# Issuing the first two weight transfers ahead of GpSimd's scaling of R of the third group, in place of behind it

## The chip, the cores and the metric

The kernel runs on one core of one Trainium2 chip. The metric is the time of one execution on the device, in microseconds (us); the number shown for a kernel is the median of several runs. Beside it stands one profiled execution, whose span runs from its first to its last recorded instruction.

The engines are named as in the profile: PE (TensorE matmul) and PEld (its weight loads), DVE (VectorE), ACT (ScalarE), POOL (GpSimd), SP (SyncE, which here only issues transfers). Each engine takes its own instructions strictly in program order.

## The reference

Two layers, one behind the other. The first is an RWKV-5 recurrence over 4 batches, 8 heads, 768 steps and 48 channels a head; the second is a two-layer network with a smooth ReLU, over 3072 tokens.

```python
# r, k, v: (4, 8, 768, 48); w, u: (8, 48)
for t in range(S):
    cur = einsum('bhd,bhe->bhde', u * k[t], v[t])
    y[t] = einsum('bhd,bhde->bhe', r[t], state + cur)
    state = w * state + einsum('bhd,bhe->bhde', k[t], v[t])
x = y.transpose(0, 2, 1, 3).reshape(3072, 384)
h = x @ w_in                                # 384 x 2048
g = where(h >= 1, h, where(h <= -1, 0, (h + 1) ** 2 / 4))
out = g @ w_out                             # 2048 x 384
```

## The kernel before

**Tiling.** The 768 steps are cut into 6 chunks of 128. A *group* is one chunk of two batches (256 tokens), so there are 12 groups, g = 0 to 11, and two *units* (one batch each) in a group: unit n belongs to group n // 2. The third group is g = 2; its units are 4 and 5. Inside a chunk the recurrence is done as matrices: K and R of a group are scaled by powers of w (steps `Ks` and `Rs`, lines 329 to 337), turned on PE (`T`, line 395), copied out of PSUM (`TT`), multiplied with one another (`A`, line 413) and masked (`AT`, lines 416 to 431). `Sp` (line 439) makes the chunk's addition to the state, `Tm` (lines 483 and 491) adds it, `Y` (lines 448 and 453) makes the output. The term with u goes its own way: `KU` (line 344), `RKU` (351), `usum` (a sum per head, 362 or 364), `V2` (376), and `y` (475) adds it to `Y`. The trace leaves numbers out of names, so the tile of `V2` shows as V in it: `V<-V,diag` at line 376 is `V2`.

The second layer takes the group's y turned (`X`, line 508; `xT`): `mm1` (line 533) multiplies with `w_in` in four quarters of 512 columns, `relu` and `square` (lines 541 and 546, ACT) and `gate` (551, DVE) make the activation, and `mm2` (561) multiplies with `w_out`.

**Order.** Nothing is scheduled by a planner. One table of tokens, `ORDER`, lists every step, and the program is written out in that order; each engine's own sequence is what the table leaves for it. A token such as `Rs.2.0@P:0` is step `Rs` of group 2, from unit 0 of the group on, on GpSimd (`@P`; `@D` is DVE, `@A` ACT), into buffer 0; `~4` puts four idle matmuls on zeros ahead of it on PE, and `warm` is idle matmuls alone. From group 2 on a step such as `Ks` or `V2` covers both units at once. A table line as it stands before the change:

```
Ks.2.0@D:0 A.3:0 Y.2:1~4 AT.1.1:1 Rs.2.0@P:0 Tm.3@D loadV.2.0:0 w_in.0 w_in.1 V2.1.0@P:0 T.5:1~8 ...
```

**Transfers.** K, R and V are loaded by SP, 384 KB for a group (line 311), in rows of 192 bytes. The weights are float32 in DRAM and bf16 on the chip, and GpSimd issues their transfers (line 297 for `w_in`, line 301 for `w_out`): `w_in.0` and `w_in.1` are columns 0 to 511 and 512 to 1023, `w_in.2` the other 1024, and `w_out.0` to `w_out.3` a quarter each. Such an issue takes GpSimd's own time, in line with its arithmetic.

**The steps around the change.** On GpSimd stand here, in this order: the masking of `AT` of unit 0 (line 423), `Rs.2.0`, the issues `w_in.0` and `w_in.1`, `V2.1.0` (group 1's first unit), the masking of `AT` of unit 1, `w_out.0`, `w_in.2`, `V2.1.1`, `KU.2.0`. DVE meanwhile does `V2.0.1`, `Tm` of unit 0, `Ks.2.0`, `Tm` of unit 3, `y.2`, `AT.3.0`. `Rs.2.0` and `Ks.2.0` are read by PE in `T.5` and `T.4`; the first reader of the weights is `mm1.0.0.0` (group 0, first quarter, unit 0), which stands on PE behind `T.5`, `T.4`, `Y.1`, two idle matmuls, `A.5`, `X.1` and `Y.3`.

Of the kernel before, what the change touches and what calls it, by code (L numbers as in the profile page):

```python
# [14 lines left out]
P = 128  # L15
# [23 lines left out]
Rs.0.1@D T.2:1~2 load.K.1.1 A.0:0 load.R.1.1 TT.2@D:1 AT.0.1:3 Sp.1:0 Tm.2@D A.2:1~2 V2.0.0@D:1 KU.1.1@D Rs.1.1@D  # L39
loadV.1.1 RKU.1.1@P AT.0.0 load.R.2.0:1 Ks.1.1@D V.1.1@A T.1:0~2 Tm.1@D usum.0.1@A Y.0:1~16 AT.2.0:0 TT.1@D:0 y.0:1  # L40
T.3:1~7 warm.6.h.2 V2.0.1@D Sp.0:0~4 usum.1.0@A:0 TT.3@A:1 A.1:2 X.0:1~4 Tm.0@D load.K.2.0:1 Sp.3:0 xT.0@A:1
Ks.2.0@D:0 A.3:0 Y.2:1~4 AT.1.1:1 Rs.2.0@P:0 Tm.3@D loadV.2.0:0 w_in.0 w_in.1 V2.1.0@P:0 T.5:1~8 sbf.1@A T.4:2~2
TT.5@A:1 AT.1.0 w_out.0 y.2:1 AT.3.0:2 w_in.2 Y.1:0~4 warm.2.h.0 A.5:1 y.1:2 usum.1.1@D X.1:1~2 Y.3:0~4 AT.5.0:0
TT.4@A:2 V2.1.1@P mm1.0.0.0:2 xT.1@A A.4:0~7 y.3:0 AT.4.0:2 X.2:1~4 load.K.3.0:2 V.2.0@A:1 xT.2@A:0 X.3:0 KU.2.0@P:1
mm1.0.0.1 mm1.0.1.0:0 w_out.2 xT.3@A mm1.0.1.1 RKU.2.0@D:0 usum.2.0@D:1 w_out.1 Sp.5:1 V2.2.0@P:1 mm1.1.1.-1:1
# [611 lines left out]
```

## Time and profile before

| | |
|---|---|
| median of 3 runs | 174.81 us (174.58 to 174.9) |
| the profiled execution | 174.86 us, span 173.1 us, granted clock 1.000 |
| busy, PE / PEld | 164.1 us (95%) / 125.7 us (73%) |
| busy, DVE / ACT / POOL | 137.5 us (79%) / 133.5 us (77%) / 111.3 us (64%) |
| moved by DMA | 28.78 MB, 166 GB/s over the span |

Rows of the timeline and of the chain of waits begin with the start and the duration in us; a bracket behind a row names how long the engine sat idle before it and what ended that. In the groups by line the three durations are the shortest, the median and the longest in ns. On PE a row's end is modelled, and rows overlap by some 0.15 us.

### The profile page before, as it was taken

The page shows a single profiled execution, that of the slowest core. Times are in us where ns is not written, and L with a number is a line of the kernel's source. Part 1 is how long each engine was busy: PE and PEld are TensorE (multiplying, and loading weights), DVE is VectorE, ACT ScalarE, POOL GpSimd, SP SyncE. Part 2 cuts the span into 40 slices and gives each one's busy share as a digit, 9 for nine tenths or more (in the row PEclk, how much of TensorE's full clock was granted, in tenths as well). Part 3 has the DMA queues.
Part 4 walks back from the last instruction along what each step waited for, and adds up shares of the span by engine and source line. Part 5 has one row for each costly group of instructions (what it writes and reads, how often), then busy time and mean ns, then how long its engine had stood idle before and what let it go on. Part 6 is the DMA issues. An engine that isn't in the chain of part 4 may idle for free.

```text
span 173.1 us, 4227 instructions
## 1 busy us (share of the span) xinstructions
PE 164.1 (95%) x1712; PEld 125.7 (73%) x1712; DVE 137.5 (79%) x175; ACT 133.5 (77%) x193; POOL 111.3 (64%) x92
## 2 busy tenths in 40 slices
PE   1989999999999999999999999999999999999992
PEld 1668879876686767686777876877769677778672
DVE  5299989899888699888998888799978795565451
ACT  4588969998659996379997997986848946898920
POOL 6487997707978479978999999999659200000000
DMA  5999999999999989799999998969999905013022
GB/s 115 210 208 232 204 191 200 182 204 213 205 167 188 202 253 201 125 196 246 153 204 205 202 223 175 229 121 207 162 253 127 139 0 140 0 45 140 0 91 91
DMA packets 107367, 28.78 MB, mean 166 GB/s; under 512 B 100946, under 2 KB 106964, under 8 KB 107348
## 3 DMA queue, kind: packets, MB, share of 16 engines
q1 hardware_dynamic: 103888, 25.24, 72.9%
q0 software_dynamic: 3312, 3.15, 11.5%
q8 instruction: 13, 0.21, 0.5%
q10 hardware_dynamic: 148, 0.13, 0.2%
q14 instruction: 6, 0.05, 0.1%
HBM read 20.45 MB, written 4.72 MB: 145 GB/s over the span
## 4 chain that ended last, share of the span: by engine, by line
PE 73%; DVE 9%; DMA 6%; SPq 4%; issue 3%; POOL 2%; ACT 1%; ACTq 0%
PE op L561 34%; PE hp L533 31%; DMA w_in_sb<-in_moe_w_in_dram 4%; SPq L311 4%; DVE gt L551 3%; PE A L413 3%; DMA R<-in_r_dram 2%; PE Y L448 2%; PE Y L453 2%; DVE Rs L334 1%; PE Sp L439 1%; POOL Rs L334 1%; DVE Tm L483 1%; DVE AT L428 1%; ACT sq L546 1%
## 5 line engine op out<-in xcount | busy, mean ns | idle before, releaser
L533 PE MATMUL hp<-xT,w_in_sb 128*128 128x256 bf16 (+1 forms) x600 | 70.1, 268 | 0.6 <-DVE AT L428 0.4
L561 PE MATMUL op<-w_out_sb,gt 128*128 128x384 bf16 (+2 forms) x400 | 69.6, 320 | 0.0
L551 DVE SCALAR_TENSOR_TENSOR gt<-sq,hp 128x1024 bf16<-128x1024 f32 x48 | 57.8, 1215 | 8.9 <-ACT sq L546 8.4
L533 PEld LDWEIGHTS <-w_in_sb 128*128 128x128 bf16 x600 | 55.4, 98 | 9.6 <-DVE gt L551 0.7
L541 ACT ACTIVATE pt<-hp 128x1024 f32<-128x1024 f32 x48 | 48.7, 1017 | 10.3 <-PE hp L533 9.7
L546 ACT ACTIVATE sq<-pt 128x1024 f32<-128x1024 f32 x48 | 50.5, 1058 | 2.9 <-DVE gt L551 2.0
L561 PEld LDWEIGHTS <-gt 128*128 128x128 bf16 x400 | 36.8, 98 | 20.4 <-DVE gt L551 0.5
L428 DVE TENSOR_TENSOR AT<-A,umask 128x1024 bf16<-128x1024 f32 x22 | 26.5, 1219 | 4.1 <-PE A L413 4.1
L351 POOL TENSOR_TENSOR RKU<-R,KU 128x768 f32<-128x768 f32 (+1 forms) x13 | 20.4, 1572 | 10.2 <-DMA R<-in_r_dram 6.3
L344 POOL TENSOR_TENSOR KU<-K,u_bc 128x768 f32<-128x768 f32 (+1 forms) x11 | 17.6, 1600 | 5.2 <-DMA K<-in_k_dram 5.2
L496 POOL TENSOR_TENSOR state<-Tm,wCm 128x384 f32<-128x384 f32 x16 | 16.8, 1053 | 1.6 <-DVE Tm L483 0.8
L334 POOL TENSOR_TENSOR Rs<-Wup,R 128x768 bf16<-128x768 f32 x9 | 16.4, 1826 | 2.1 <-DMA R<-in_r_dram 2.1
L334 POOL TENSOR_TENSOR Ks<-Wdn,K 128x768 bf16<-128x768 f32 x9 | 16.4, 1824 | 1.5 <-PE Sp L439 1.5
L376 POOL TENSOR_TENSOR V<-V,diag 128x768 f32<-128x768 bf16 (+1 forms) x11 | 15.3, 1390 | 2.8 <-DVE diag L364 2.4
L212 ACT COPY oo<-op 128x384 f32<-128x384 f32 x18 | 8.5, 473 | 10.7 <-PE op L561 9.2
L475 DVE TENSOR_TENSOR yy<-Y,V 128x384 bf16<-128x384 f32 x18 | 9.7, 553 | 3.8 <-PE Y L453 3.0
L453 PE MATMUL Y<-V,AT 128*128 128x48 bf16 x192 | 11.0, 183 | 0.3 <-POOL AT L423 0.3
L483 DVE TENSOR_TENSOR Tm<-Sp,state 128x384 f32<-128x384 f32 x16 | 8.8, 552 | 2.9 <-PE Sp L439 2.5
L364 DVE TENSOR_REDUCE diag<-RKU 128x16 f32<-128x768 f32 (+1 forms) x12 | 10.5, 879 | 0.0
L453 PEld LDWEIGHTS <-AT 128*128 128x128 bf16 x192 | 9.4, 96 | 1.5 <-issue 0.5
L216 ACT CAST V<-VF 128x768 bf16<-128x768 f32 (+1 forms) x11 | 8.1, 739 | 0.7 <-DMA VF<-in_v_dram 0.7
L448 PE MATMUL Y<-state_bf,RT 128*128 128x96 bf16 x72 | 8.5, 204 | 0.0
(85 smaller groups left out, 143.8 us busy)
## 6 DMA issues: line engine op xcount, KB each, us to landing
out_dram<-oo SPq DMA_DIRECT2D x11, 384.0 KB, 3.5
R<-in_r_dram SPq DMA_DIRECT2D x10, 384.0 KB, 4.4
K<-in_k_dram SPq DMA_DIRECT2D x10, 384.0 KB, 6.0
VF<-in_v_dram SPq DMA_DIRECT2D x10, 384.0 KB, 5.2
w_out_sb<-in_moe_w_out_dram POOLq DMA_DIRECT2D x4, 384.0 KB, 8.3
K<-in_k_dram SPq DMA_DIRECT2D x4, 192.0 KB, 3.7
R<-in_r_dram SPq DMA_DIRECT2D x4, 192.0 KB, 3.5
VF<-in_v_dram SPq DMA_DIRECT2D x4, 192.0 KB, 3.8
```

What stands on the lines that cost most here:

```text
L334: engines[e].tensor_mul(of_unit(dst, j0, j1)[:, :, :, :D], rep(tab, j1 - j0), of_unit(tiles[what, g], j0, j1))
L344: engines[e].tensor_mul(of_unit(tiles["KU", g], j0, j1), of_unit(tiles["K", g], j0, j1), rep(u_bc, j1 - j0))
L351: engines[e].tensor_mul(of_unit(tiles["RKU", g], j0, j1), of_unit(tiles["R", g], j0, j1), of_unit(tiles["KU", g], j0, j1))
L376: engines[e].tensor_mul(tiles["V2", g][:, hs, :], tiles["V", g][:, hs, :], tiles["diag", g][:, hs].unsqueeze(2).to_broadcast([P, hs.stop - ...
L428: nc.vector.tensor_mul(t.rearrange("p i n t -> p (i n) t"), tiles.pop(("A", n)).rearrange("p i n t -> p (i n) t"), umask.unsqueeze(1).to_b ...
L453: nc.tensor.matmul(t[:, 2 * p + i, :], tiles["AT", n][:, i, p, :], tiles["V", g][:, j * H + 2 * p + i, :], start=(c == 0), stop=True, skip ...
L496: nc.gpsimd.tensor_mul(states[(g % BP) * UNITS + j], tiles.pop(("Tm", n)), wCm)
L533: nc.tensor.matmul(hp[:, f, cols], w_in_sb[:, i, n0 : n0 + P], tiles["xT", g][:, units, i, :], start=(i == 0), stop=(i == nK - 1), skip_gr ...
L541: nc.scalar.activation(tiles["pt", g, q], tiles["hp", g, q], AF.Relu, bias=0.5, scale=0.5)
L546: nc.scalar.activation(tiles["sq", g, q], tiles.pop(("pt", g, q)), AF.Square, bias=0.0)
L551: nc.vector.scalar_tensor_tensor(out=gt, in0=tiles.pop(("sq", g, q)), scalar=1.0, in1=tiles.pop(("hp", g, q)), op0=ALU.min, op1=ALU.max)
L561: nc.tensor.matmul(t, tiles["gt", g, q][:, f, j * P : (j + 1) * P], w_out_sb[:, n, cols], start=(n == 0), stop=(n == nF - 1),)
```

## The change

The two tokens `w_in.0 w_in.1` move ahead of `Rs.2.0@P:0` in the table; of the 715 tokens in it no other is altered. `Tm.3@D` (DVE) and `loadV.2.0:0` (SP), which stood between, belong to other engines and keep their places there.

```diff
-Ks.2.0@D:0 A.3:0 Y.2:1~4 AT.1.1:1 Rs.2.0@P:0 Tm.3@D loadV.2.0:0 w_in.0 w_in.1 V2.1.0@P:0 T.5:1~8 sbf.1@A T.4:2~2
+Ks.2.0@D:0 A.3:0 Y.2:1~4 AT.1.1:1 w_in.0 w_in.1 Rs.2.0@P:0 Tm.3@D loadV.2.0:0 V2.1.0@P:0 T.5:1~8 sbf.1@A T.4:2~2
```

GpSimd, from the masking of unit 0 to that of unit 1 (`V_411<-V,diag` is `V2.1.0`); the difference of the two programs:

```order
 L423 AFFINE_SELECT AT<-AT 128x1024
+L297 DMA w_in_sb<-in_moe_w_in_dram 128x3x512 x2
 L334 TENSOR_TENSOR Rs<-Wup,R 128x16x48
-L297 DMA w_in_sb<-in_moe_w_in_dram 128x3x512 x2
 L376 TENSOR_TENSOR V_411<-V,diag 128x384
 L423 AFFINE_SELECT AT<-AT 128x1024
```

The two issues and `Rs.2.0` have changed places; what follows them is as it was. DVE over the same stretch, with what each row waits for; it reads alike in both programs (`V_247` is `V2` of group 0, the rows of line 491 are `Tm`, the row of line 334 is `Ks.2.0`):

```order
L475 TENSOR_TENSOR y<-Y,V_247 128x384 [waits DVE_49,PE_49]
L376 TENSOR_TENSOR V_247<-V,diag 128x384 [waits Activation_49]
L491 TENSOR_TENSOR state<-Sp,wCm 128x384 [waits PE_49]
L334 TENSOR_TENSOR Ks<-Wdn,K 128x16x48 [waits DMAHW7_49]
L491 TENSOR_TENSOR state<-Sp,wCm 128x384 [waits PE_49]
L475 TENSOR_TENSOR y<-Y,V_411 128x384 [waits DVE_49,PE_49,Pool_49]
L428 TENSOR_TENSOR AT<-A,umask 128x1024
```

Nothing moved on DVE, and `Ks.2.0` waits for its load of K and for no other engine; `y.2`, two rows on, waits for GpSimd's `V2.1.0`. On PE, ACT and SP too both programs have the same rows.

## The prediction

> **What bounds the kernel now.** I read the page first, then the chain of waits, then the waits of the stretch from 20 to 24.5 us, and last the timelines around the change. From the page, the shares of busy time and the chain by engine; from the chain in order of time, one piece; from the waits, one line:
>
> ```profile
> core 0: 173.1 us, clock 1.000
> PE 164.1 (95%) x1712; PEld 125.7 (73%) x1712; DVE 137.5 (79%) x175; ACT 133.5 (77%) x193; POOL 111.3 (64%) x92
> PE 73%; DVE 9%; DMA 6%; SPq 4%; issue 3%; POOL 2%; ACT 1%; ACTq 0%
> 17.66 6.09 DMA w_in_sb<-in_moe_w_in_dram
> PEld L533 <- DMA w_in_sb<-in_moe_w_in_dram: 0.2, 1, 0.2
> ```
>
> PE is 95% busy and holds 73% of the chain. The chain also runs through 6.09 us of the first weight transfer, issued behind `Rs.2.0`, which makes it look as if every microsecond of an earlier issue were won. The waits say otherwise: PE's weight load stood 0.2 us for this transfer. The chain names who came last; the wait says by how much. So 0.20 us is all that an earlier landing can give directly, however early it is.
>
> **What GpSimd does, and whom it holds up.** The timeline of POOL, then of DVE, then of PE; line 423 is the masking, line 376 `V2`:
>
> ```profile
> 15.89 1.83 POOL L334 TENSOR_TENSOR Rs<-Wup,R 128x768 bf16<-128x768 f32 x1
> 17.66 1.70 POOL L297 DMA_DIRECT2D w_in_sb<-in_moe_w_in_dram  x2
> 19.38 1.14 POOL L376 TENSOR_TENSOR V<-V,diag 128x384 f32<-128x384 bf16 x1
> 20.49 1.08 POOL L423 TENSOR_SCALAR_AFFINE_SELECT AT<-AT 128x1024 bf16<-128x1024 bf16 x1
> 23.25 0.83 POOL L376 TENSOR_TENSOR V<-V,diag 128x384 f32<-128x384 bf16 x1 [0.18 <-DVE diag L364]
> ...
> 12.78 0.55 DVE L376 TENSOR_TENSOR V<-V,diag 128x384 f32<-128x384 bf16 x1
> 17.31 0.82 DVE L376 TENSOR_TENSOR V<-V,diag 128x384 f32<-128x384 bf16 x1
> 18.14 0.56 DVE L491 TENSOR_TENSOR state<-Sp,wCm 128x384 f32<-128x384 f32 x1
> 18.62 1.22 DVE L334 TENSOR_TENSOR Ks<-Wdn,K 128x768 bf16<-128x768 f32 x1
> 20.55 0.56 DVE L475 TENSOR_TENSOR y<-Y,V 128x384 bf16<-128x384 f32 x1 [0.25 <-POOL V L376]
> 21.03 1.22 DVE L428 TENSOR_TENSOR AT<-A,umask 128x1024 bf16<-128x1024 f32 x1
> 26.55 0.95 DVE L351 TENSOR_TENSOR RKU<-R,KU 128x768 f32<-128x768 f32 x1
> ...
> 17.77 0.33 PE L439 MATMUL Sp<-V,Ks 128*128 128x96 bf16 x4
> 20.37 0.39 PE L395 MATMUL T<-ident,Ks 128*128 128x128 bf16 x4
> 20.59 0.39 PE L395 MATMUL T<-ident,Rs 128*128 128x128 bf16 x4
> 21.63 0.37 PE L453 MATMUL Y<-V,AT 128*128 128x48 bf16 x8
> 22.30 0.29 PE L615 MATMUL idle<-zeros 128*128 128x128 bf16 x2 [0.30 <-DVE AT L428]
> 23.79 0.84 PE L533 MATMUL hp<-xT,w_in_sb 128*128 128x128 bf16 x12
> ```
>
> Two things are to be seen. GpSimd has no gap from 15.89 on. And the same `V2` of 128x384 takes DVE 0.55 us at 12.78 and 0.82 us at 17.31, where GpSimd's `Rs.2.0` runs until 17.72; on GpSimd it takes 0.83 us at 23.25 and 1.14 us at 19.38, where DVE's `Ks.2.0` runs until 19.84. So the two get in each other's way where both read two tensors from SBUF. The clearest rows stand later, with what PE does there; from SP's timeline the load of R for group 3, and from the page's transfers its kind:
>
> ```profile
> 27.52 0.37 SPq L311 DMA_DIRECT2D R<-in_r_dram x1
> ...
> R<-in_r_dram SPq DMA_DIRECT2D x10, 384.0 KB, 4.4
> ...
> 39.89 1.82 POOL L351 TENSOR_TENSOR RKU<-R,KU 128x768 f32<-128x768 f32 x1 [6.29 <-DMA R<-in_r_dram]
> 41.68 1.70 POOL L496 TENSOR_TENSOR state<-Tm,wCm 128x384 f32<-128x384 f32 x1
> ...
> 40.16 2.37 DVE L334 TENSOR_TENSOR Rs<-Wup,R 128x768 bf16<-128x768 f32 x1
> 42.45 1.21 DVE L551 SCALAR_TENSOR_TENSOR gt<-sq,hp 128x1024 bf16<-128x1024 f32 x1
> ...
> 42.78 0.81 PE L561 MATMUL op<-w_out_sb,gt 128*128 128x384 bf16 x4
> 43.72 1.48 PE L533 MATMUL hp<-xT,w_in_sb 128*128 128x256 bf16 x12
> 43.71 1.21 PEld L533 LDWEIGHTS <-w_in_sb 128*128 128x128 bf16 x12 [0.51 <-DVE gt L551]
> 45.20 0.65 PE op L561 x4
> ```
>
> DVE's `Rs.3.0` begins 0.27 us behind GpSimd's `RKU.3.0` and ends at 42.53, 0.82 behind that one's end at 41.71: it took 2.37 us where a product of this size takes 0.95 (the row at 26.55). It stood until GpSimd was through. And GpSimd, with its next step ready at 41.7, stood in turn until DVE was through. Whoever begins first keeps the other out to its end, and one that stands waiting gets its turn ahead of the other's next step.
>
> **The change, part by part.** All times are in the profiled execution.
>
> *The issues.* They begin at 15.89 in place of 17.66, 1.77 us earlier, and take 1.70 us: until 17.59. `w_in.0` then lands between 23.75 − 1.77 = 21.98, if its queue is no longer, and 23.75, if it only waits longer behind the loads of SP. Either will do, as the last step shows.
>
> *`Rs.2.0`* moves behind them. DVE's `V2.0.1` now begins first, at 17.31, beside issues alone, for 0.55 us: until 17.86. GpSimd comes free of such a wait about 0.15 us ahead of the row's end on DVE (its `V2` at 19.38 takes 1.14 in place of 0.83, so it really began at 19.69, and `Ks.2.0` ends at 19.84). `Rs.2.0` so runs from 17.71 for 1.83 us, to 19.54. PE reads it at 20.59: this delay in itself costs nothing, since 1.05 us of cover are left of 2.9.
>
> *`Ks.2.0` on DVE* is where it costs. The 0.27 us that `V2.0.1` saves do not help: `Tm` behind it waits for `Sp` on PE, which ends at 17.77 + 0.33 = 18.10, so `Tm` stays at 18.14 and `Ks.2.0` at 18.62. There it now meets `Rs.2.0` in place of the issues, and ends 0.82 us behind it: 20.36 in place of 19.84, +0.52 us.
>
> *What is queued behind.* GpSimd's `V2.1.0` would begin at 19.5 but waits for `Ks.2.0`: 20.36 − 0.15 + 0.83 = 21.04, against 20.52. Both engines behind it: the masking ends at 22.12, so PE's `Y.1` begins at 22.14, not 21.63; and `y.2` on DVE, which already stands 0.25 us for `V2.1.0`, begins at 21.07, so `AT.3.0` ends at 22.77, not 22.25. PE's idle matmuls at 22.30 stand for that `AT`: 22.82. (`T.5` needs `Ks.2.0` at 20.37, just in time; a little lateness there lies inside the wait of `Y.1`.) PE is +0.52 here, and gives back the 0.20 us for the weights at `mm1.0.0.0`: 23.79 + 0.52 − 0.20 = 24.11, later than both landings. Net +0.32 us.
>
> *The bound from above.* `Ks.2.0` took 1.22 us beside issues alone, where 0.95 would be its price alone. I don't know what the 0.27 us are. If an issue adds as much to `V2.0.1`, this ends at 18.13 as before, and all of the above is 0.27 later: +0.59 us. I take +0.43, halfway, as neither row is nearer.
>
> Here a rule of the Trainium skill, "SBUF — State Buffer", section "Who interferes with whom", differs from the row. It says that a DVE instruction with two SBUF inputs contends with a GpSimd instruction that reads SBUF, as a lock held for the whole instruction, and infers that writing transfer descriptors does not collide with it. By that rule the sum would be +0.32, by the row at 18.62 +0.59; the lock itself agrees with the 2.37 us at 40.16.
>
> *Whether it reaches the end.* From 24 to 43 us each step hangs on PE's `A.4` behind `mm1.0.0.0`, and PE, ACT and DVE shift together. But at 43.72 PE waits for DVE's `gate`, which stands behind `Rs.3.0`, which stands behind `RKU.3.0`, which began when R of group 3 landed, at 39.89. That does not hang on PE: DVE may arrive at 40.16 + 0.43 and still end at 42.53. PE's spare time here is between 43.72 − (42.78 + 0.65) = 0.29 and the weight load's 0.51; I take 0.40. So the end moves by the larger of 0.43 − 0.40 = 0.03 and the shift of that landing. The landing came 12.37 us after the issue at 27.52, against a median of 4.4: 8 us of it are queue behind the weights. The issue follows `RKU.2.0` on DVE (26.55 + 0.95) and so is up to 0.43 late (0.32 to 0.59 by the bounds); the queue in front is as long as before. The shift is thus between 0, if the queue sets it, and all of the delay; I take 0.1, near the queue's end, since 8 of 12 us are queue.
>
> **Sum:** −0.20 (weights) + 0.52 to 0.79 (`Ks.2.0`, `V2.1.0`, `AT.3.0`) − 0.40 (absorbed at 43.72), but not less than the landing's shift: +0.1 us. On the profiled execution's 174.86 that is 174.96; on the median, 0.05 below it, 174.9.
>
> **The rivals.** 0.2% is 0.35 us, about what a measurement of this kernel tells from no change.
>
> *Slower: the delay is carried through.* If R of group 3 lands as late as it is issued, or if GpSimd gets `V2.1.0` in ahead of the waiting `Ks.2.0` (0.83 us more for DVE, PE +1.15), the end moves: +0.32 to 0.59 by the first, +0.75 by the second even with 0.40 absorbed. Time 175.2 to 175.6. It decides from a landing over 0.35 us late, or PE over 0.75 late at `mm1.0.0.0`. For it: the issue of that load does hang on DVE. Against it: the 8 us of queue, and the order of turns at 41.7.
>
> *Faster: no collision.* If `Ks.2.0` is not held, it ends at 18.62 + 0.95 = 19.57, `V2.1.0` at 19.38 + 0.83 = 20.21, `AT.3.0` 0.3 us earlier, and the 0.20 us for the weights is won too: PE −0.2 to −0.5. The end follows only as far as R of group 3 lands earlier: 174.3 to 174.6. Against it: three pairs of rows that show the two engines blocking one another.
>
> *Nothing moves:* the weights are sent no earlier, because they stand behind SP's loads. `mm1.0.0.0` is due at 24.11 and they land at 23.75 at the latest, so the time is that of the forecast.
>
> **How the numbers follow.** The forecast, within 0.35 us of before, has 0.51 (its own range 174.5 to 175.15); the slower rival 0.32, since three steps in a row carry the delay and only one wait absorbs it; the faster one 0.17, which includes that the transfers sort themselves better than the rows tell. The range, 174.3 to 175.6, reaches over most of both, and leaves about 2 in 10 out.
>
> **What would show it.** Right: `V2.0.1` 0.55 us; `Rs.2.0` ending at about 19.5; `Ks.2.0` at about 1.75 us in place of 1.22; no wait of PE for the weights; a longer wait of PE at `Y.1` and ahead of the idle matmuls; `mm1.0.0.0` at 24.1 to 24.4; `RKU.3.0` still at about 39.9. The prediction is wrong if `Ks.2.0` is no longer than before, if `RKU.3.0` moves by more than 0.35 us, or if DVE's `Rs.3.0` gets ahead of `RKU.3.0` (then it takes 0.95, and PE's wait at 43.72 goes).

## The result, and the profile after

The changed kernel takes 175.56 us (median of 20 runs, 175.18 to 177.43), the kernel before 174.90 in the same comparison (20 runs, 174.41 to 175.94): a ratio of 1.0053 (95% interval 1.0031 to 1.0075), slower by some 0.5%. The prediction's 174.9 was "no change". The profiled execution of the changed kernel took 176.90 us. It is one of 6 among its 20 with a granted clock of 0.988 to 0.990 and times of 176.6 to 177.4 us; the other 14 lie between 175.2 and 175.7, so the loss is not that of those 6 alone.

From the page of the changed kernel, the busy shares and the clock in 40 slices; ahead of them the span and mean clock:

```profile
core 0: 175.2 us, clock 0.989
PE 165.2 (94%) x1712; PEld 126.8 (72%) x1712; DVE 137.6 (79%) x175; ACT 133.8 (76%) x193; POOL 112.0 (64%) x92
PEclk9999969999999999999999999999999999999999
```

Busy times are within 0.3 us of before on DVE and ACT; PE and PEld are 1.1 us longer, at a lower clock in the sixth slice (21.9 to 26.3 us), and POOL 0.7. The timeline around the change, POOL, then DVE, then PE:

```profile
15.75 1.70 POOL L297 DMA_DIRECT2D w_in_sb<-in_moe_w_in_dram  x2
17.48 1.82 POOL L334 TENSOR_TENSOR Rs<-Wup,R 128x768 bf16<-128x768 f32 x1
19.25 1.15 POOL L376 TENSOR_TENSOR V<-V,diag 128x384 f32<-128x384 bf16 x1
...
17.19 2.52 DVE L376 TENSOR_TENSOR V<-V,diag 128x384 f32<-128x384 bf16 x1
19.64 0.54 DVE L491 TENSOR_TENSOR state<-Sp,wCm 128x384 f32<-128x384 f32 x1
20.11 1.11 DVE L334 TENSOR_TENSOR Ks<-Wdn,K 128x768 bf16<-128x768 f32 x1
...
20.24 0.34 PE L439 MATMUL Sp<-V,Ks 128*128 128x96 bf16 x4 [1.42 <-ACT AT L419]
```

`V2.0.1` on DVE takes 2.52 us, not 0.55. It began 0.29 us ahead of `Rs.2.0`, and yet ended 0.41 behind it: less its own 0.55, it got going at 19.16, 0.14 ahead of the end of the other's row. `Rs.2.0` was ready all that time: its load of R, the last thing that it waited for, had been issued at 10.82 and took 4.7 us to land, so from about 15.5 on nothing but the steps ahead of it on GpSimd kept it. The hand-over then goes on in turn, each time with 0.13 to 0.14: `V2.1.0` on GpSimd (19.25 + 1.15 = 20.40, so going from 19.57, when `V2.0.1` was through at 19.71), then `Ks.2.0` on DVE (ends 21.22, going from 20.27). Before, `Ks.2.0` ended at 19.84.

On PE stands a wait of 1.42 us at the second `Sp`, that of unit 3. The timeline names ACT's `AT` for it; the waits of 15 to 26 us name what the weight load behind the same point waited for:

```profile
PEld L439 <- DVE state L491: 1.6, 1, 1.6
PE Sp L439 <- ACT AT L419: 1.4, 1, 1.4
```

DVE's `state` at line 491 is `Tm` of unit 0, which reads the PSUM tile that this `Sp` writes next. `Tm` stood behind `V2.0.1` in DVE's order: 19.64 in place of 18.14. The windows of this kernel (length, then busy time of PE, PEld, DVE, ACT, POOL, then the clock) show what followed:

```profile
19.00:21.20 2.20, 0.96 (x21) 0.78 (x22) 2.20 (x4) 1.66 (x3) 2.20 (x3) 1.00 1.18 191
21.20:25.00 3.80, 3.80 (x51) 3.70 (x50) 2.12 (x5) 1.74 (x2) 2.47 (x3) 0.55 1.21 188
...
22.00:23.00 1.00, 1.00 (x12) 1.00 (x11) 1.00 (x2) 0.00 (x0) 1.00 (x3) 0.50 1.20 189
```

In this execution PE ran at half its clock for about 3.4 us behind the gap (an estimate: at 0.50 or 1.00 throughout, a mean of 0.55 over 3.80 us takes 3.4 us at 0.50), and `mm1.0.0.0` began at 26.18. There was no wait for `w_in` any more.

### The profile page after: what moved, and what is told of

It reads as the page before. It is cut to its first block, busy times and chain, and to the rows that moved or that the text cites. A ratio compares the mean times of both kernels' runs of the same rounds, so it can differ in the third digit from the quotient of the medians.

```text
span 175.2 us, 4227 instructions
## 1 busy us (share of the span) xinstructions
PE 165.2 (94%) x1712; PEld 126.8 (72%) x1712; DVE 137.6 (79%) x175; ACT 133.8 (76%) x193; POOL 112.0 (64%) x92
## 4 chain that ended last, share of the span: by engine, by line
PE 86%; DVE 4%; ACT 3%; issue 2%; POOL 1%; DMA 1%; ACTq 0%
PE op L561 36%; PE hp L533 33%; PE A L413 4%; PE Y L453 2%; PE Y L448 2%; PE T L395 2%; PE Sp L439 2%; PE T L204 1%; DMA u_row<-in_u_dram 1%; PE ub L249 1%; PE wc L284 1%; PE wb L244 1%; DVE AT L428 1%; DVE gt L551 1%; ACT sq L546 1%
## 5 line engine op out<-in xcount | busy, mean ns | idle before, releaser
L334 POOL TENSOR_TENSOR Ks<-Wdn,K 128x768 bf16<-128x768 f32 x9 | 17.1, 1901 | 1.9 <-PE Sp L439 1.9
L496 POOL TENSOR_TENSOR state<-Tm,wCm 128x384 f32<-128x384 f32 x16 | 16.0, 1006 | 1.9 <-DVE Tm L483 1.2
```

The costliest lines, as they stand in the source:

```text
L334: engines[e].tensor_mul(of_unit(dst, j0, j1)[:, :, :, :D], rep(tab, j1 - j0), of_unit(tiles[what, g], j0, j1))
L496: nc.gpsimd.tensor_mul(states[(g % BP) * UNITS + j], tiles.pop(("Tm", n)), wCm)
```

## The experiments

The first theory of what had happened: `V2.0.1` is held by `Rs.2.0` from the time on at which that stands ready behind the issues, and the loss is what hangs on that. The rivals: DVE came too late, by a fraction of a microsecond, to go first; the issues themselves hold DVE; the order on DVE (`Tm` behind `V2.0.1`) is the loss; the earlier weight traffic is; the lower clock is. To compare traces, the start of `mm1.0.0.0` is counted from the start of GpSimd's masking of unit 0 (line 423), the step ahead of the change. It is 23.79 − 14.83 = 8.96 us in the trace of before.

| kernel | ratio to before [95%] | median | `V2.0.1` | `Ks.2.0` | `mm1.0.0.0` |
|---|---|---|---|---|---|
| changed, again | 1.0024 [1.0002, 1.0045] | 176.03 | 2.53 | 1.11 | 9.89 |
| changed, again_2 | 1.0016 [0.9993, 1.0038] | 175.74 | 2.53 | 1.11 | 9.89 |
| before_again | 0.9992 [0.9962, 1.0021] | 175.17 | 1.37 | 1.11 | 9.93 |
| tm_first | 1.0006 [0.9985, 1.0027] | 175.77 | 0.57 | 1.58 | 9.89 |
| three_issues | 1.0064 [1.0038, 1.0090] | 176.55 | 1.08 | 2.24 | 9.91 |
| rs_late | 1.0004 [0.9972, 1.0035] | 175.84 | 0.56 | 0.95 | 10.01 |
| v2_early | 1.0076 [1.0049, 1.0104] | 176.26 | 3.00 | 0.94 | 10.37 |
| one_ahead | 1.0014 [0.9994, 1.0034] | 175.30 | 1.76 | 1.61 | 9.62 |
| rs_buffer | 0.9975 [0.9952, 0.9998] | 175.12 | 0.55 | 1.73 | 9.25 |

They ran on three chips, on which the kernel before took 175.44 (again, tm_first, three_issues, rs_late), 174.97 (v2_early, v2_w3, slot, one_ahead) and 175.31 us (rs_buffer, before_again, warm, again_2); medians compare only within a chip. The diffs are against the changed kernel.

**The changed kernel once more (again),** unaltered, beside the next three.

> The changed kernel once more, unaltered. In its first profile V2.0.1 on DVE (line 376) takes 2.52 us from 17.19, to the end of Rs.2.0 on GpSimd, Tm of unit 0 waits behind it, and PE stands 1.59 us for Tm's PSUM bank ahead of Sp.3; from 21.2 to 24.3 us the granted clock is 0.5. Theory of the port: the 2.52 us and PE's gap of about 1.6 us stand in every execution, and cost 0.5 to 0.9 us in time by themselves (175.4 to 175.8). Theory of the clock: the loss is the lowered clock, and an execution at clock 1.000 loses nothing against before (174.6 to 175.1). Expected: a profile or runs at clock 1.000 with 175.5 us, and some runs near 176.8 with clock 0.99.

Slower again, by 0.24%. Its profiled execution kept the clock (0.998), which separates the two parts of the loss. GpSimd, DVE, PE with its weight load, and in a fence of its own a piece of the chain from 30 to 45 us:

```profile
18.00 1.82 POOL L334 TENSOR_TENSOR Rs<-Wup,R 128x768 bf16<-128x768 f32 x1
...
17.71 2.53 DVE L376 TENSOR_TENSOR V<-V,diag 128x384 f32<-128x384 bf16 x1
...
20.64 1.11 DVE L334 TENSOR_TENSOR Ks<-Wdn,K 128x768 bf16<-128x768 f32 x1
...
43.88 1.22 DVE L551 SCALAR_TENSOR_TENSOR gt<-sq,hp 128x1024 bf16<-128x1024 f32 x1 [0.77 <-PE op L561]
...
20.77 0.34 PE L439 MATMUL Sp<-V,Ks 128*128 128x96 bf16 x4 [1.34 <-DVE state L491]
...
42.31 2.11 PE L561 MATMUL op<-w_out_sb,gt 128*128 128x384 bf16 x12 [0.20 <-DMA w_out_sb<-in_moe_w_out_dram]
...
45.15 1.21 PEld L533 LDWEIGHTS <-w_in_sb 128*128 128x128 bf16 x12 [0.30 <-DVE gt L551]
```

```profile
34.12 8.15 DMA w_out_sb<-in_moe_w_out_dram
```

The hold on `V2.0.1` and PE's gap are the same to 0.1 us; here the gap's releaser is named as `Tm`. Further on PE waits 0.20 us for the last quarter of `w_out`, which GpSimd issued at 34.12 and which took 8.15 us to land. In the trace of before that issue went out at 32.80, and nothing waited for it. The weight load's wait for `gate`, 0.51 us at 43.71 before, is 0.30 here; and `gate` itself, which waited for nobody before, waits 0.77 us for PE.

**`Tm` ahead of `V2.0.1` on DVE (tm_first).**

```diff
-T.3:1~7 warm.6.h.2 V2.0.1@D Sp.0:0~4 usum.1.0@A:0 TT.3@A:1 A.1:2 X.0:1~4 Tm.0@D load.K.2.0:1 Sp.3:0 xT.0@A:1
+T.3:1~7 warm.6.h.2 Sp.0:0~4 usum.1.0@A:0 TT.3@A:1 A.1:2 X.0:1~4 Tm.0@D V2.0.1@D load.K.2.0:1 Sp.3:0 xT.0@A:1
```

> The changed kernel with Tm.0 ahead of V2.0.1 on DVE, so that what waits for GpSimd's port no longer stands ahead of what PE waits for. If the loss is the way V2.0.1 -> Tm.0 -> PSUM bank -> Sp.3: Tm.0 begins at about 18.0, Sp.3 on PE at about 18.7 (before: 18.77) with no gap over 0.3 us, V2.0.1 is held from about 18.5 to 19.7, Ks.2.0 ends at 20.5 to 20.7, and the time is 174.6 to 175.1, with no run at a lower clock. If the loss comes from the early transfers themselves (their traffic, or Rs.2.0 late for PE), the time stays at 175.4 to 175.7.

PE's gap at `Sp` is gone, but `mm1.0.0.0` comes no earlier. POOL, then DVE, then PE:

```profile
17.51 1.82 POOL L334 TENSOR_TENSOR Rs<-Wup,R 128x768 bf16<-128x768 f32 x1
19.29 1.15 POOL L376 TENSOR_TENSOR V<-V,diag 128x384 f32<-128x384 bf16 x1
21.00 1.21 POOL L423 TENSOR_SCALAR_AFFINE_SELECT AT<-AT 128x1024 bf16<-128x1024 bf16 x1 [0.56 <-ACT AT L419]
...
19.18 0.57 DVE L376 TENSOR_TENSOR V<-V,diag 128x384 f32<-128x384 bf16 x1
19.68 1.58 DVE L334 TENSOR_TENSOR Ks<-Wdn,K 128x768 bf16<-128x768 f32 x1
...
21.32 0.40 PE L395 MATMUL T<-ident,Ks 128*128 128x128 bf16 x4 [0.22 <-DVE Ks L334]
```

`V2.0.1` is through at 19.75, `V2.1.0` at 20.44, `Ks.2.0` at 21.26: counted from the masking, `Ks.2.0` ends at 6.51, as in again (20.64 + 1.11 − 15.24 = 6.51). So PE's gap is one place where the delay shows, not its source. `Rs.2.0`, `V2.0.1`, `V2.1.0` and `Ks.2.0` go one behind the other whatever the order on DVE. Before, `Ks.2.0` had the issues to run beside; now DVE has nothing of this kind for them. The ratio is back to 1.0006, though its interval overlaps that of again. Behind `mm1.0.0.0` the one thing that its trace has ahead of again's is that the last quarter of `w_out`, issued at 33.63, keeps nobody waiting; the run warm below has the same and is slower, so this trace does not explain the ratio.

**A third issue ahead of `Rs.2.0` (three_issues).**

```diff
-Ks.2.0@D:0 A.3:0 Y.2:1~4 AT.1.1:1 w_in.0 w_in.1 Rs.2.0@P:0 Tm.3@D ...
-TT.5@A:1 AT.1.0 w_out.0 y.2:1 AT.3.0:2 w_in.2 ...
+Ks.2.0@D:0 A.3:0 Y.2:1~4 AT.1.1:1 w_in.0 w_in.1 w_out.0 Rs.2.0@P:0 Tm.3@D ...
+TT.5@A:1 AT.1.0 y.2:1 AT.3.0:2 w_in.2 ...
```

> The changed kernel with w_out.0 also issued ahead of Rs.2.0: issues from 15.75 to 18.25, and Rs.2.0 from there to 20.1. V2.0.1 on DVE begins at about 17.2, in the second issue, as in the changed kernel. Theory A (GpSimd's next arithmetic instruction claims the port as soon as its own waits are met, while the one issue ahead of it is still being written; an issue itself holds nobody): the second issue is followed by a third one, so V2.0.1 takes 0.55 us, PE has no gap ahead of Sp.3, and Ks.2.0 at 18.6 is held to 20.1 and ends at about 20.9. Theory B (the writing of a transfer's descriptors holds a DVE instruction with two SBUF inputs): V2.0.1 is held at least to the end of the third issue at 18.25, over 1.0 us, or to the end of Rs.2.0 at 20.1 (3.3 us), and then the time is 176 or more.

POOL and DVE:

```profile
17.57 0.78 POOL L301 DMA_DIRECT2D w_out_sb<-in_moe_w_out_dram  x1
18.37 1.82 POOL L334 TENSOR_TENSOR Rs<-Wup,R 128x768 bf16<-128x768 f32 x1
...
17.31 1.08 DVE L376 TENSOR_TENSOR V<-V,diag 128x384 f32<-128x384 bf16 x1
18.78 2.24 DVE L334 TENSOR_TENSOR Ks<-Wdn,K 128x768 bf16<-128x768 f32 x1
```

`V2.0.1` lost 0.53 us and then went ahead of `Rs.2.0`: it got going at 17.84, 0.27 into the third issue. This fits neither a claim that holds from the first issue on nor free passage beside issues. `Ks.2.0` then met `Rs.2.0` and took 2.24 us, and the last quarter of `w_out`, issued as late as 37.70, held PE as well. Slower by 0.6%.

**Another GpSimd step behind the issues (rs_late):** `V2.1.0`, whose sums ACT has not finished by then, with `Rs.2.0` behind it.

```diff
-... w_in.0 w_in.1 Rs.2.0@P:0 Tm.3@D loadV.2.0:0 V2.1.0@P:0 T.5:1~8 ...
+... w_in.0 w_in.1 Tm.3@D loadV.2.0:0 V2.1.0@P:0 Rs.2.0@P:0 T.5:1~8 ...
```

> The changed kernel with Rs.2.0 behind V2.1.0 on GpSimd: issues from 15.75 to 17.45, then V2.1.0, which has to wait for ACT's sums until about 18.0, then Rs.2.0. Theory A (the next arithmetic instruction claims the port once its own waits are met): at 17.2 the waits of V2.1.0 are not met, so V2.0.1 takes 0.55 us and PE has no gap ahead of Sp.3. Theory B (the issue itself holds DVE): V2.0.1 is held to 17.45 at least, 0.7 to 0.8 us, as Ks.2.0 took 1.22 in place of 0.95 before. Rs.2.0 ends at about 21, so PE's T.5 waits some 0.4 us and the time is 174.8 to 175.4 by either.

POOL, DVE, PE:

```profile
16.23 1.70 POOL L297 DMA_DIRECT2D w_in_sb<-in_moe_w_in_dram  x2
19.17 1.52 POOL L376 TENSOR_TENSOR V<-V,diag 128x384 f32<-128x384 bf16 x1 [1.24 <-ACT RKU L362]
...
17.66 0.56 DVE L376 TENSOR_TENSOR V<-V,diag 128x384 f32<-128x384 bf16 x1
19.05 0.95 DVE L334 TENSOR_TENSOR Ks<-Wdn,K 128x768 bf16<-128x768 f32 x1
...
22.52 0.40 PE L395 MATMUL T<-ident,Rs 128*128 128x128 bf16 x4 [0.86 <-POOL Rs L334]
```

Beside the same two issues `V2.0.1` now runs free, 0.56 us, and `Ks.2.0`, behind them, takes its bare 0.95. So these two issues did not hold `V2.0.1` by themselves; what stood behind them did. The kernel gains nothing by it, as PE waits 0.86 us for `Rs.2.0`, which is late here.

**`V2.0.1` earlier on DVE, ahead of `y.0` (v2_early),** to see whether DVE only came too late.

```diff
-... Y.0:1~16 AT.2.0:0 TT.1@D:0 y.0:1
-T.3:1~7 warm.6.h.2 V2.0.1@D Sp.0:0~4 ...
+... Y.0:1~16 AT.2.0:0 TT.1@D:0 V2.0.1@D y.0:1
+T.3:1~7 warm.6.h.2 Sp.0:0~4 ...
```

> The changed kernel with V2.0.1 one place earlier on DVE, ahead of y.0, so that it begins at about 16.7, some 0.7 us ahead of Rs.2.0, in the first 0.1 us of the second issue. Theory A (GpSimd's next arithmetic instruction claims the port some time into the issue ahead of it, and an instruction of DVE that begins before that goes first): V2.0.1 takes 0.55 to 0.85 us, PE has no gap ahead of Sp.3, and the rest goes as the prediction had it: Rs.2.0 ends at 19.4, Ks.2.0 is held from 18.6 and ends at 20.2 to 20.4, mm1.0.0.0 begins at 24.0 to 24.5, time within 0.2% of before. Rival (DVE with two SBUF inputs is held through the whole run of issues and Rs.2.0, however early it begins): V2.0.1 takes 2.9 us or more, y.0 and Tm.0 wait behind it, and the time is 0.3% to 0.7% above before.

POOL, DVE, PE:

```profile
16.11 1.70 POOL L297 DMA_DIRECT2D w_in_sb<-in_moe_w_in_dram  x2
17.84 1.82 POOL L334 TENSOR_TENSOR Rs<-Wup,R 128x768 bf16<-128x768 f32 x1
...
17.08 3.00 DVE L376 TENSOR_TENSOR V<-V,diag 128x384 f32<-128x384 bf16 x1
...
20.60 0.38 PE L204 MATMUL X<-zeros 128*128 128x128 bf16 x4 [1.66 <-DVE y L475]
```

It began 0.76 us ahead of `Rs.2.0` and was held to that one's end all the same: 17.08 + 3.00 − 0.55 = 19.53, 0.13 ahead of 19.66. Being first on the clock does not help DVE here. The ratio is the second worst, 1.0076.

**As v2_early, and with the last quarter of `w_out` issued ahead of `Ks.3.0` (v2_w3),** to take away the wait for it.

```diff
-... relu.0.2:0 square.0.2:1 Ks.3.0@P:2 KU.3.0@D:1
-... gate.0.3:0 w_out.3 mm1.1.3.-1:0 Rs.3.0@D:2
+... relu.0.2:0 square.0.2:1 w_out.3 Ks.3.0@P:2 KU.3.0@D:1
+... gate.0.3:0 mm1.1.3.-1:0 Rs.3.0@D:2
```

> As v2_early, and w_out.3 is issued ahead of Ks.3.0 on GpSimd, 1.8 us earlier. In the profile of the changed kernel on this chip PE stood 0.43 us at 42.31 for the landing of w_out.3, issued at 34.12. If that issue sets the landing: w_out.3 lands 1 to 1.8 us earlier, PE has no wait there, and the time is 0.1% to 0.3% below v2_early. If the traffic in front of it sets the landing (its queue still works off w_out.1 when it comes): the landing moves by less than 0.5 us and the time is that of v2_early.

1.0103 [1.0061, 1.0145], median 177.38. Four of its six executions had a clock of 0.988 to 0.990 (177.3 to 177.6 us), the other two took 175.76 and 176.15. From its windows, and then from the timeline of PE:

```profile
21.00:25.00 4.00, 4.00 (x53) 3.71 (x51) 2.81 (x4) 2.36 (x4) 2.57 (x3) 0.57 1.11 188
```

```profile
20.38 0.38 PE L204 MATMUL X<-zeros 128*128 128x128 bf16 x4 [1.93 <-DVE y L475]
```

With executions of two kinds, the run says nothing on `w_out`; nor does the trace of v2_early have a wait for `w_out` that could be taken away (PE's wait in again was 0.20 us, not 0.43, and on another chip). It does repeat the pairing of a PE gap near 2 us with half the clock for the next 3 to 4 us.

**One issue ahead, one behind (one_ahead).**

```diff
-... w_in.0 w_in.1 Rs.2.0@P:0 Tm.3@D loadV.2.0:0 V2.1.0@P:0 T.5:1~8 ...
+... w_in.0 Rs.2.0@P:0 Tm.3@D loadV.2.0:0 w_in.1 V2.1.0@P:0 T.5:1~8 ...
```

> The changed kernel with w_in.0 alone ahead of Rs.2.0 and w_in.1 behind it: Rs.2.0 from 16.6 to 18.45. V2.0.1 on DVE begins in the middle of it at about 17.2 and is held to its end by both theories, 1.6 us in place of 2.52; Tm.0 ends at about 19.3, PE's gap ahead of Sp.3 is 0.6 to 0.8 us in place of 1.5, and the time is between before and the changed kernel, 0.1% to 0.3% above before. If the loss were in the number of bytes sent early, half of it would remain whatever V2.0.1 does.

1.0014, not told from no change. Here `Rs.2.0` began ahead of `V2.0.1` (16.80 against 17.30), and `V2.0.1` was held to its end (16.80 + 1.83 = 18.63), as the prediction's rule has it; PE stood 0.66 us at `Sp`, about half of the 1.34 to 1.43 of the changed kernel, and `mm1.0.0.0` came 0.66 us later than in the trace of before.

**`w_in.0` in an earlier idle slot of GpSimd (slot),** ahead of `RKU.1.1`, `w_in.1` where it was before.

```diff
-loadV.1.1 RKU.1.1@P AT.0.0 load.R.2.0:1 ...
-... AT.1.1:1 w_in.0 w_in.1 Rs.2.0@P:0 Tm.3@D loadV.2.0:0 V2.1.0@P:0 ...
+loadV.1.1 w_in.0 RKU.1.1@P AT.0.0 load.R.2.0:1 ...
+... AT.1.1:1 Rs.2.0@P:0 Tm.3@D loadV.2.0:0 w_in.1 V2.1.0@P:0 ...
```

> The kernel before, with w_in.0 issued in GpSimd's idle time of 1.34 us ahead of RKU.1.1 (12.5 to 13.9), and w_in.1 left behind Rs.2.0. Nothing on GpSimd is delayed by the issue there. If an early landing is worth only PE's 0.2 us: Rs.2.0 at 15.9 as before, V2.0.1 0.8 us as before, V2.1.0 0.9 us earlier, PE's wait for the weights gone, time 0 to 0.2% below before. If the early traffic itself harms (it goes in front of the loads of K and V for group 2): Ks.2.0 on DVE or T.5 on PE wait for K, and the time is 0.2% to 0.8% above before.

1.0025 [0.9997, 1.0054]. The profiled execution, 177.14 us, is its slowest, and has waits that the others have not. POOL and DVE:

```profile
16.81 1.82 POOL L334 TENSOR_TENSOR Rs<-Wup,R 128x768 bf16<-128x768 f32 x1 [0.64 <-DMA R<-in_r_dram]
...
21.79 0.96 DVE L334 TENSOR_TENSOR Ks<-Wdn,K 128x768 bf16<-128x768 f32 x1 [2.28 <-DMA K<-in_k_dram]
```

The loads of R and K of group 2 land late, with the weights issued ahead of them; that the weights are the cause is not shown by this one trace. In the changed kernel, which issues them 3 us later, no such wait is seen.

**`Rs.2.0` into another buffer (rs_buffer):** the changed kernel, but buffer 1 is read by PE's `T.3` (whose rows on PE end about when `V2.0.1` begins: 16.85 + 0.39 = 17.24 against 17.16 below), so that `Rs.2.0` is not free to start until shortly before the issues end.

```diff
-... AT.1.1:1 w_in.0 w_in.1 Rs.2.0@P:0 Tm.3@D ...
+... AT.1.1:1 w_in.0 w_in.1 Rs.2.0@P:1 Tm.3@D ...
```

> The changed kernel with Rs.2.0 written into buffer 1 in place of 0. Buffer 1 is read last by PE's T.3, some 3.5 us after RKU.1.1 begins on GpSimd (17.4 in the first profile), so Rs.2.0 becomes ready only shortly before the issues end, and after V2.0.1 has begun on DVE (3.4 us). Nothing else differs. Readiness theory (an arithmetic instruction of GpSimd that is ready while the issues ahead of it are still being written keeps DVE's two-input instructions off the port from then on): V2.0.1 takes 0.55 to 0.85 us; Rs.2.0 runs from about 3.9 to 5.7 us after that anchor; Ks.2.0 is held to its end, as the prediction had it; mm1.0.0.0 begins 0.3 to 0.6 us later against the anchor than before, not 0.9; the time is within 0.25% of before. Rival (issues followed by Rs.2.0 hold DVE whatever it waits for): V2.0.1 takes 2.5 us again and the time is 0.3% to 0.6% above before.

Faster than the changed kernel beside it: 175.12 us against the 175.74 of again_2, a ratio of 0.9965, and nine of its twelve executions lie below the fastest of again_2 (175.30). Against the kernel before it is barely ahead, 0.9975 [0.9952, 0.9998], with medians of 175.12 and 175.31. POOL, DVE, PE, then the weight load behind PE's wait at 44 us:

```profile
15.72 1.70 POOL L297 DMA_DIRECT2D w_in_sb<-in_moe_w_in_dram  x2
17.45 1.94 POOL L334 TENSOR_TENSOR Rs<-Wup,R 128x768 bf16<-128x768 f32 x1
19.35 1.54 POOL L376 TENSOR_TENSOR V<-V,diag 128x384 f32<-128x384 bf16 x1
...
17.16 0.55 DVE L376 TENSOR_TENSOR V<-V,diag 128x384 f32<-128x384 bf16 x1
18.00 0.56 DVE L491 TENSOR_TENSOR state<-Sp,wCm 128x384 f32<-128x384 f32 x1 [0.29 <-PE Sp L439]
18.48 1.73 DVE L334 TENSOR_TENSOR Ks<-Wdn,K 128x768 bf16<-128x768 f32 x1
...
16.85 0.39 PE L395 MATMUL T<-ident,Rs 128*128 128x128 bf16 x4
...
23.93 0.83 PE L533 MATMUL hp<-xT,w_in_sb 128*128 128x128 bf16 x12
...
44.05 1.21 PEld L533 LDWEIGHTS <-w_in_sb 128*128 128x128 bf16 x12 [0.56 <-DVE gt L551]
```

The instructions, their engines and their order are those of the changed kernel; only the moment from which `Rs.2.0` may start differs. `V2.0.1` runs free, and what the prediction forecast for this stretch is here: `Rs.2.0` to 19.39 (19.54 forecast), `Ks.2.0` to 20.21 (20.36), `V2.1.0` to 20.89 (21.04), which is exact when counted from the masking, as that began 0.15 us earlier here; `mm1.0.0.0` at +0.29 (+0.32 by its lower bound); and PE's wait for `gate` near 44 us is there as before. Why it comes out ahead of the kernel before, this trace does not say; the next run may.

**The kernel before once more (before_again).**

> The kernel before, unaltered, for a second profile. It tells how far the marks used in the comparison vary by themselves: the begin of mm1.0.0.0, of the mm1 behind Rs.3.0, and the end, each counted from the begin of RKU.1.1 on GpSimd (before: 9.9, 29.8 and 159.2 us). Expected within 0.3 us of these. If they vary by 0.7 us or more, the shifts of the other kernels of that size are no evidence.

Its time is that of before, 0.9992, but not its trace. POOL, DVE, PE:

```profile
16.40 1.82 POOL L334 TENSOR_TENSOR Rs<-Wup,R 128x768 bf16<-128x768 f32 x1 [0.52 <-PE Y L453]
18.17 1.70 POOL L297 DMA_DIRECT2D w_in_sb<-in_moe_w_in_dram  x2
...
17.27 1.37 DVE L376 TENSOR_TENSOR V<-V,diag 128x384 f32<-128x384 bf16 x1
...
24.72 0.68 PE L533 MATMUL hp<-xT,w_in_sb 128*128 128x128 bf16 x9 [0.70 <-DMA w_in_sb<-in_moe_w_in_dram]
```

`Rs.2.0` started 0.52 us late. The row names PE's `Y`, but in the other trace `Rs.2.0` began at 15.89, ahead of that `Y` (15.98); its other wait, the load of R, is left. That load was issued at 11.13 and took 5.1 us here, so it landed at 16.23; in the first trace it was issued at 11.34 and took 4.4, and landed at 15.74. The issues behind it slid along, and PE waited 0.70 us for the weights, where the first trace had 0.20. `mm1.0.0.0` is at 9.93, as late as in the changed kernel. Kernels that issue ahead of `Rs.2.0` don't hang on that load there; this may be where rs_buffer is ahead of before, but no run shows it by itself. So marks of single traces of the kernel before differ by 0.97 us, and differences of that size between two traces prove little; what I rest on are the holds within each trace and the timed ratios.

**Idle matmuls in PE's gap (warm),** 24 of them ahead of `Sp.3`, to keep the clock up.

```diff
-... Tm.0@D load.K.2.0:1 Sp.3:0 xT.0@A:1
+... Tm.0@D load.K.2.0:1 warm.24.h.0 Sp.3:0 xT.0@A:1
```

> The changed kernel with 24 idle matmuls (1.3 us) on PE ahead of Sp.3, where PE otherwise stands 1.5 us for Tm's PSUM bank. Theory of the gap: the lowered clock that 7 of 20 executions of the changed kernel showed (clock 0.988 to 0.990 in the mean, 176.6 to 177.4 us, against 175.2 to 175.7 at clock 0.997 to 1.000) follows PE's gap; with the gap filled no execution is below 0.995, and the time is that of the changed kernel's executions at clock 1.000, 0.3% to 0.4% above before. Rival: the lowered clock comes by chance or from the traffic, and is as frequent as in the unaltered changed kernel beside it.

1.0038 [1.0016, 1.0060]: 176.03 us, and `V2.0.1` at 2.53 as in the changed kernel. The lower clock had come in 6 of the first 20 executions, not 7. No execution of these 12 is under a clock of 0.997, but of the changed kernel beside it (again_2) only one in 12 was, so this shows little of the clock. It does show that the loss stays without the lower clock, with a reservation: its profiled execution has a wait of PE of 0.61 us at 85 us, for a transfer that turns y into `xT`, which no other trace here has. That trace has no wait for `w_out`.

**And the changed kernel beside these (again_2).**

> The changed kernel, unaltered, on the same chip as the two above, as their control. V2.0.1 2.5 us again, PE's gap 1.5 us, mm1.0.0.0 0.9 us later against the anchor than before; 0.25% to 0.6% above before, and more where executions show a clock of 0.99.

1.0016 [0.9993, 1.0038]. Rows as in again: `V2.0.1` 2.53 us, PE's wait 1.43 us for `Tm`, the last quarter of `w_out` issued at 33.82 and 8.18 us under way, with PE waiting 0.20 for it.

## Why the prediction was wrong

**The step that failed** is the first one on GpSimd and DVE: "`V2.0.1` now begins first, at 17.31, beside issues alone, for 0.55 us: until 17.86." It did begin first, and took 2.52 to 2.53 us in all three profiles of the changed kernel. The rule behind it, "whoever begins first keeps the other out to its end", was drawn from a pair in which GpSimd had begun first. rs_buffer settles what was wrong with it: with the same instructions in the same order, and `Rs.2.0` not free to start until about when `V2.0.1` begins, `V2.0.1` takes 0.55 us and the kernel gains. `Rs.2.0`'s place was not the trouble; that it already stood ready behind the issues was. v2_early takes away the rival that DVE was late by a little (0.76 us ahead, 3.00 us long), rs_late that the issues themselves hold DVE.

**What hung on it.** "`Tm` stays at 18.14 and `Ks.2.0` at 18.62" fell with it: 19.64 and 20.11. `Ks.2.0` did not meet `Rs.2.0` but `V2.1.0`, and lost only 0.16 us to it; it began 1.49 us later (20.11 in place of 18.62). PE was due +0.32 to +0.59 at `mm1.0.0.0`; the two traces of the changed kernel at full clock have +0.93 by the trace of before, and −0.04 by that of before_again, so this size is uncertain and the loss rests on the timed ratios. I had put the possibility of a longer hold into the bound of 0.27 us, "if an issue adds as much", and so had sized it by the wrong row; the hold measured 1.97 (2.52 − 0.55).

**The absorption at 43.72**, put at 0.40 us, was too large a term. It held only as long as `gate` on DVE was later than PE; in again `gate` itself waits 0.77 us for PE, and the weight load's wait for `gate` is then 0.30 us, as it also is in before_again. Counted from the masking, that weight load starts at 28.88 us in the trace of before, at 29.54 and 29.55 in tm_first and warm, and at 29.91 and 29.94 in again and again_2. All four have `mm1.0.0.0` at +0.93. So about 0.27 us were absorbed in tm_first and warm, and nothing in again and again_2, where PE also waits 0.20 us for the last quarter of `w_out`. The prediction asked whether the landing of R hangs on PE, and not what else GpSimd issues in that stretch: this quarter goes out behind steps that move with PE (33.82 and 34.12, against 32.80) and is 8.2 us under way. Yet the wait for it is not needed for a loss: v2_early and warm have none and are slower by 0.8 and 0.4%.

So the 0.51 on "no change" rested on a step that failed and a term that was too large. The time came out where the slower rival had it (175.2 to 175.6), and that is luck in the main. PE was over 0.75 us late at `mm1.0.0.0`, as the rival says, and `V2.1.0` did go ahead of `Ks.2.0`, but because `Ks.2.0` itself came late, and not because it was passed over while it waited. The landing of R for group 3 did not decide either: by the start of `RKU.3.0` it came at 39.49 in again and at 42.30 in again_2 (41.85 in before_again), and PE's first wait was the same `w_out` in again and again_2.

**What was right.** The 0.20 us for the weights were won: no trace of the changed kernel has a wait for `w_in`. The trace of before_again shows that 0.20 was one execution's number, though; it can be 0.70. `V2.1.0`, `Ks.2.0` and `AT.3.0` carry a delay to PE as described. And by rs_buffer the sizes of the sum were good once `V2.0.1` goes first.

The rule of the Trainium skill that the prediction weighed ("SBUF — State Buffer", section "Who interferes with whom") holds in one half. Writing descriptors did not by itself hold DVE's product of two SBUF inputs: 0.55 and 0.56 us beside issues in rs_buffer and rs_late. The other half, that the order of issue decides who blocks, gave the wrong result here if it is read by the starts of the rows: v2_early's DVE row starts 0.76 us first and is blocked for 2.45.

**What stays open.** A GpSimd product that stands ready behind an issue held DVE to its end in the changed kernel, v2_early, v2_w3 and warm. But in the trace of before `V2.1.0` had its last sum from ACT at 18.12, stood behind `w_in.1`, and `Ks.2.0`, which began at 18.62, still went first, with 0.27 us lost; and in three_issues `V2.0.1` went first after 0.53. Readiness was needed for the hold in these runs; it was not enough. The starts nearly sort by the last issue ahead of the GpSimd product: DVE products that began 0.04 to 0.52 us behind the start of that issue were held, and two that began ahead of it (by 0.26 in three_issues, and `Ks.2.0` in before_again by 0.07) went first. But `Ks.2.0` of the first trace of before, 0.04 behind it, went first too, so what decides stays open. Nor is the lower clock settled: it came in 6 of 20, 0 of 12 and 1 of 12 executions of the changed kernel in three comparisons, each 1 to 2 us longer than the rest. Of the profiles only the first of the changed kernel and that of v2_w3 have it, behind PE gaps of 1.42 and 1.93 us; again, again_2 and v2_early have gaps of 1.34 to 1.66 us and kept the clock.

## What to carry to other kernels

An early start of one instruction is not a free slot: before moving a GpSimd step behind a block of issues, ask whether it will stand there ready, and what DVE wants to read from two SBUF tensors meanwhile; if so, let its buffer or its data come free only when the issues end, which cost one digit here and made the kernel 0.35% faster than the changed one on the same chip. Work that two engines cannot do side by side adds up whatever its order, so look for what can run beside the issues and leave that there. And take an absorbing wait for certain only after every transfer that moves with the delay has been followed to its reader.

## What the runs showed of the hardware

- In the changed kernel, v2_early, v2_w3 and warm a DVE product of two SBUF inputs that started 0.28 to 0.76 us ahead of a GpSimd product was blocked to that one's end, while the latter stood ready behind the descriptor-writing of a transfer (2.52 to 3.00 us in place of 0.55). In three_issues and in the kernel before such a product went first, after 0.53 and 0.27 us, so this is no rule. The hand-over comes 0.12 to 0.14 us ahead of the end of the blocking row in every trace that has it.
- PE's granted clock fell to 0.50 for about 3.4 us behind a gap of 1.42 us, in part of the executions. The Trainium skill, "TensorE: Matmul & The Clock Gate", Part 1, speaks of a window of about 3.4 us that runs freely: an idle one closes the gate and a busy one opens it. The length of the slow stretch agrees with a busy window, but the gap that was enough here was under half of an idle one.
- In two executions of the kernel before, the load of R for group 2 landed at 15.74 and 16.23 us, and `mm1.0.0.0`, counted from the masking, began 0.97 us apart; the two took 174.86 and 175.56 us.
